# Naming PSUM pairs by a rough clock and ordering an attention stage by a plan string, in a fused attention and sine-MLP kernel

## The chip, the cores and the metric

One core of a Trainium2 chip. The metric is the device time of one execution in microseconds (us), the median of several runs; before: 469.61 us (469.1 to 469.65, 3 runs). A trace of one execution comes with each kernel; its span is some 2 us shorter than the timed run. Engine names: PE is TensorE, ACT ScalarE, DVE VectorE, POOL GpSimd, SP SyncE. The granted clock is the share of its full rate that TensorE was given, as the profile shows it; half clock is 0.50.

## The reference, cut to what matters

```python
def _attn_ref(q, k, v, g_q, g_k):            # 8 batches, 12 heads, 448 tokens, head width 64
    q_n, k_n = rmsnorm(q, g_q), rmsnorm(k, g_k)
    attn = softmax(q_n @ k_n.T / sqrt(64))
    return attn @ v
def _moe_ref(x, w_in, w_out, alpha):         # x: 3584 tokens x 768; 2048 hidden
    h = x @ w_in
    s = np.sin(alpha * h)
    g = h + s * s / (alpha + 1e-09)
    return g @ w_out
```

## The kernel before

For each batch there is an attention phase, then a first product (96 matmuls, 18.3 us; ACT, POOL and DVE turn it into g). The second product of batch b-1 has no attention of its own to wait for and is cut into steps that fill the attention phase of batch b on PE. Batch 0 has nothing to fill with and uses dummy matmuls.

The order of instructions is set by hand. All PSUM tiles (PSUM is the memory that this kernel's matmuls write to) are pairs of banks from one pool, in turn:

```python
psum = ctx.enter_context(tc.tile_pool(name="ps", bufs=4, space=bass.MemoryType.PSUM))
def bank_pair(name):
    return psum.tile([P, 2, 512], F32, tag="ps", name=name)
```

A score step S takes a pair until ACT has made the exponential; a value step A takes one until the denominator (two ACT passes) and the normalisation xT (two DVE multiplies) are done; an output tile takes one for 16 filler steps F and then until DVE has copied it out.

```python
def scores(c, j, warm=0):
    sc = bank_pair("sc")
    ...                                                     # 4 matmuls
    nc.scalar.activation(expT[c, j], sc[:, :, :S], ACT.Exp, scale=SCALE)
def attend(pi):
    av = bank_pair("av")
    ...                                                     # 28 matmuls: 7 key tiles, values and ones
    nc.scalar.activation(rec, av[:, 1, :S], ACT.Ln)
    nc.scalar.activation(rec, rec, ACT.Exp, scale=-1.0)
    ...                                                     # DVE: xT = av * rec, two halves
```

And the next batch's queries and keys are normed inside the attention phase, a chain over three engines and the DMA: squares and gain on POOL (steps 0, 1, 2), two reductions on DVE (3, 4), the inverse norm on ACT and the scaling on POOL (5), a transposing DMA (6). The list `at` says at which slot of the phase each step is issued; two such chunks run one after the other in a phase.

The softmax here doesn't subtract the row's maximum and nothing guards it: scores larger than these inputs give would overflow.

Of the kernel before, what the change touches and what calls it, by code (L numbers as in the profile page):

```python
# [32 lines left out]
def kernel(  # L33
# [38 lines left out]
    BUSY = (20, 8, 4, 2, 2)  # L72
# [10 lines left out]
    epool = ctx.enter_context(tc.tile_pool(name="expT", bufs=14))  # L83
# [5 lines left out]
    psum = ctx.enter_context(tc.tile_pool(name="ps", bufs=4, space=bass.MemoryType.PSUM))  # L89

    def bank_pair(name):
        return psum.tile([P, 2, 512], F32, tag="ps", name=name)
# [53 lines left out]
    def spread_g():  # L146

        nc.gpsimd.tensor_mul(g_rows[:, 2], g_rows[:, 0], g_rows[:, 1])
        ps = bank_pair("gps")
        nc.tensor.matmul(ps[:, 0, :D], ones_row, g_rows[:, 2], start=True, stop=True)  # L150
        nc.scalar.copy(gg[:, 0], ps[:, 0, :D])  # L151

    def spread_alpha():

        ps = bank_pair("aps")
        nc.tensor.matmul(ps[:, 0, :MT], small, ident_f32, start=True, stop=True)
        nc.vector.tensor_copy(alpha_sb[:, :, 0], ps[:, 0, :MT])
        nc.vector.reciprocal(inv_alpha_sb, alpha_sb)
# [12 lines left out]
    def keep_busy(n, rhs):  # L171


        ps = bank_pair("ps")
        for _ in range(n):
            nc.tensor.matmul(ps[:, 0, :rhs.shape[-1]], blank[:, :P], rhs, start=True, stop=True)

    qkT, expT, xT = {}, {}, {}

    def norm_tasks(ci):  # L180
# [6 lines left out]
        st.inv = {}  # L187
# [17 lines left out]
        def rsqrt(ws=slice(0, 2)):  # L205
            ln = npool.tile([P, 2, 2 * NJ], F32, tag="inv", name="inv")
            inv = bank_pair("inv")[:, :, :2 * NJ] if early else ln
            for w in range(2)[ws]:
                st.inv[w] = inv[:, w, :]
            nc.scalar.activation(ln[:, ws], st.ms[:, ws, :], ACT.Ln, scale=1.0 / D, bias=eps)  # L210
            nc.scalar.activation(inv[:, ws], ln[:, ws], ACT.Exp, scale=-0.5)

        def scale(w):
            eng = nc.vector if early else nc.gpsimd
            if st.n is None:
                st.n = npool.tile([P, 2, NJ, 2, D], BF16, tag="qkn", name="qkn")
            n, x = st.n[:, w], qk[ci][:, w].rearrange("p (hi j) d -> p hi j d", hi=2)
            inv = st.inv[w].rearrange("p (hi j) -> p hi j", hi=2)
            for hi in range(2):
                eng.tensor_mul(n[:, :, hi, :], x[:, hi], inv[:, hi].unsqueeze(2).to_broadcast([P, NJ, D]))  # L220

# [8 lines left out]
        def pe_transpose(pairs, ws=(0, 1), act=False):  # L230
            tp = psum.tile([P, 2, 1024], BF16, tag="ps", name="tp")
            for pp in pairs:
                pi, r = 2 * ci + pp, slice(pp * 64, pp * 64 + 64)
                if pi not in qkT:
                    qkT[pi] = tpool.tile([P, 2, S], BF16, tag="qkT", name="qkT")
                for w in ws:
                    for j in range(NJ):
                        c = w * S + j * REST
                        nc.tensor.transpose(tp[:, pp, c:c + REST], st.n[r, w, j], ident[r, r])
            for pp in pairs:  # L240
                out = qkT[2 * ci + pp][:, ws[0]:ws[-1] + 1].rearrange("p w s -> p (w s)")
                src = tp[:, pp, ws[0] * S:(ws[-1] + 1) * S]
                if act:
                    nc.scalar.copy(out, src)
                else:
                    nc.vector.tensor_copy(out, src)

# [6 lines left out]
    def scores(c, j, warm=0):  # L254

        sc = bank_pair("sc")
        for _ in range(warm):
            nc.tensor.matmul(sc[:, 0], blank[:, :P], blank, start=True, stop=True)
        for pp in range(2):
            for hi in range(2):  # L260
                qkt, r = qkT[2 * c + pp], slice(hi * 64, hi * 64 + 64)
                nc.tensor.matmul(sc[key_rows(pp, hi), pp, :S], qkt[r, 1, j * REST:(j + 1) * REST], qkt[r, 0, :],  # L262
                                 start=True, stop=True)
        expT[c, j] = epool.tile([P, 2, S], BF16, tag="expT", name="expT")
        nc.scalar.activation(expT[c, j], sc[:, :, :S], ACT.Exp, scale=SCALE)  # L265

    def attend(pi):
# [16 lines left out]
        for hi in range(2):  # L284
            r, o = slice(hi * 64, hi * 64 + 64), slice(64 - hi * 64, 128 - hi * 64)
            nc.vector.tensor_mul(xT[b][r, hp, :], av[r, 0, :S], rec[o, :])  # L286

    def snake(b, hps, m):
# [8 lines left out]
        def finish():  # L297
            nc.vector.scalar_tensor_tensor(  # L298
                g_sb[:, m, (b % 2) * S:(b % 2 + 1) * S], s2, inv_alpha_sb[:, m, :], hps, op0=ALU.mult, op1=ALU.add)
        return finish  # L300

    def first_product(b, beside):
# [10 lines left out]
        tiles = {}  # L313
        for kts in (range(KT - 2), [KT - 2], [KT - 1]):
            for i in range(EARLY):
                if i not in tiles:
                    tiles[i] = bank_pair("hps")
                for m in (2 * i, 2 * i + 1):
                    mm(tiles[i], m, kts)
        for i in range(MT // 2):  # L320
            if i >= EARLY:
                tiles[i] = bank_pair("hps")
                for m in (2 * i, 2 * i + 1):
                    mm(tiles[i], m, range(KT))
            for m in (2 * i, 2 * i + 1):
                late.append(snake(b, tiles[i][:, m % 2, :S], m))
# [4 lines left out]
        while late:  # L331
            late.popleft()()

    def second_product(b):
# [9 lines left out]
        for i, halves in units:  # L344
            st = {}

            def step(m, i=i, halves=halves, st=st):
# [4 lines left out]
                for k, half in enumerate(halves):  # L352
                    nc.tensor.matmul(st["ps"][:, k, :HALF], lhsT, w_out_sb[:, m, half * HALF:(half + 1) * HALF],  # L353
                                     start=(m == 0), stop=(m == MT - 1))
                if m == MT - 1:
                    n = len(halves)
                    osb = opool.tile([P, 2, HALF], F32, tag="osb", name="osb")
                    nc.vector.tensor_copy(osb[:, :n], st["ps"][:, :n, :HALF])  # L358
                    o = osb[:, :n].rearrange("p a d -> p (a d)")
# [51 lines left out]
    def beside_h(b):  # L411

        ci = NC * b + 5
        if ci >= NC * B:
            return {}
        return {0: [lambda: begin_norm(ci)], 1: [step_of(ci, 0)], 3: [step_of(ci, 1)], 4: [step_of(ci, 3)],
                5: [step_of(ci, 2)], 7: [step_of(ci, 4)]}

    FIRST, KEPT = 12, MT // 2
    for c in range(NC):  # L420
        for j in range(NJ):
            scores(c, j, BUSY[2 + c] if j % 2 else 0)
            if c and j in (1, 3):
                attend(2 * c - 2 + j // 2)
            if (c, j) == (0, 1):
                c1.rsqrt()
            if (c, j) == (0, 3):
                c2.square(0), c2.square(1)
                c2.fold_g()
                c1.scale(0), c1.scale(1)  # L430
                load_qk(NC)
            if (c, j) == (0, 4):
                c1.pe_transpose((0, 1))
                c2.reduce(0), c2.reduce(1)
            if (c, j) == (1, 0):
                c2.rsqrt()
                c2.scale(0), c2.scale(1)
                load_qk(NC + 1)
                load_w_out(0)
                begin_norm(NC)  # L440
                step_of(NC, 0, 1, 2)()
            if (c, j) == (1, 4):
                c2.pe_transpose((0, 1))
                step_of(NC, 3, 4)()
                v_parts = load_v(1)
                v_parts[0](), v_parts[1]()
                begin_norm(NC + 1)
                step_of(NC + 1, 0, 1, 2)()
            if (c, j) == (1, 6):
                step_of(NC, 5, 6)()  # L450
            if (c, j) == (2, 1):
                step_of(NC + 1, 3, 4)()
                v_parts[2](), v_parts[3]()
                load_w_out(1)
            if (c, j) == (2, 4):
                step_of(NC + 1, 5)()
    step_of(NC + 1, 6)()
    attend(NP - 2)
    attend(NP - 1)
    first_product(0, beside_h(0))  # L460

    visits = [(c, *x) for c in range(NC) for x in (((0, 1), 0), ((2, 3), 1), ((4, 5, 6), None))]
    for b in range(1, B):
        nc.scalar.preload_act_table_set(EXP_LN)
        fillers.extendleft(reversed(second_product(b - 1)))

        n_fill = len(fillers) - (KEPT if b % 2 == 0 else 0)

        at = [[] for _ in range(4 * NP + 8)]
# [3 lines left out]
        step_of(ci, 5)()  # L473
        at[s0].append(step_of(ci, 6))
# [8 lines left out]

        def beside_e(v, half):
            a, z = v * 4 * NP // len(visits), (v + 1) * 4 * NP // len(visits)
            mid = (a + z) // 2
            for slot in range(a, mid) if half == 0 else range(mid, z):
                for task in at[slot]:
                    task()

        fill(FIRST // 2 if b > 1 else 0)
        for n, (c, tiles, pp) in enumerate(visits):
            for j in tiles:
                scores(b * NC + c, j)
            if n == 0:
                fill(FIRST - (FIRST // 2 if b > 1 else 0))
            elif c and pp is not None:
                attend(b * NP + 2 * c - 2 + pp)
            beside_e(n, 0)
            left = n_fill - FIRST  # L500
            fill(left * (n + 1) // len(visits) - left * n // len(visits))
            beside_e(n, 1)
        attend(b * NP + NP - 2)
        attend(b * NP + NP - 1)
        for task in [task for slot in at[4 * NP:] for task in slot]:
            task()
# [31 lines left out]
```

## Time and profile before

| part of the span | us | PE idle in it |
|---|---|---|
| attention phase of batch 0, from the start | 45.6 | 8.0 after its first 13.9 us |
| attention phase of batch 1 | 34.9 | 3.9 |
| attention phases of batches 2 to 7, each | 35.7 | 2.1 |
| first products, each | 18.3 | none |
| last second product and store | 25.1 | at its end |

Read it as: PE is the bound, the first products are full, so only the attention phases can shrink. The lines are in the prediction. The phase lengths in this document are taken from the first and last first-product matmul in the timelines.

### The profile page before, as it was taken

The page shows a single profiled execution, that of the slowest core. Times are in us where ns is not written, and L with a number is a line of the kernel's source. Part 1 is how long each engine was busy: PE and PEld are TensorE (multiplying, and loading weights), DVE is VectorE, ACT ScalarE, POOL GpSimd, SP SyncE. Part 2 cuts the span into 40 slices and gives each one's busy share as a digit, 9 for nine tenths or more (in the row PEclk, how much of TensorE's full clock was granted, in tenths as well). Part 3 has the DMA queues.
Part 4 walks back from the last instruction along what each step waited for, and adds up shares of the span by engine and source line. Part 5 has one row for each costly group of instructions (what it writes and reads, how often), then busy time and mean ns, then how long its engine had stood idle before and what let it go on. Part 6 is the DMA issues. An engine that isn't in the chain of part 4 may idle for free.

```text
span 466.7 us, 9464 instructions
## 1 busy us (share of the span) xinstructions
PE 433.9 (93%) x3815; PEld 220.3 (47%) x3820; DVE 227.5 (49%) x331; ACT 342.8 (73%) x531; POOL 278.2 (60%) x262
## 2 busy tenths in 40 slices
PE   7768999899999999999999999999999999999996
PEld 2334544445544554445544555445544455445563
DVE  3764563537453473445545365435634464224521
ACT  4879877868876788767887688767887588876800
POOL 3868968828785368836788187854688276001400
PEclk9999999999999999999999999999999999999999
DMA  6999996490257905583055904668052901211023
GB/s 237 192 244 239 230 198 203 146 187 17 62 134 162 180 2 151 154 99 132 4 160 146 225 2 54 179 134 169 2 153 74 126 25 25 50 37 50 1 50 86
DMA packets 69296, 55.09 MB, mean 118 GB/s; under 512 B 41460, under 2 KB 65796, under 8 KB 69252
## 3 DMA queue, kind: packets, MB, share of 16 engines
q1 hardware_dynamic: 56690, 40.97, 34.6%
q0 software_dynamic: 11616, 11.81, 18.1%
q10 hardware_dynamic: 946, 1.70, 1.0%
q8 instruction: 30, 0.49, 0.4%
q14 instruction: 14, 0.11, 0.1%
HBM read 45.62 MB, written 11.01 MB: 121 GB/s over the span
## 4 chain that ended last, share of the span: by engine, by line
PE 66%; ACT 16%; DMA 6%; DVE 5%; issue 4%; POOL 2%; SPq 1%; DVEq 0%; POOLq 0%
PE hps L309 27%; PE ops L353 25%; ACT expT L265 11%; PE av L277 9%; PE sc L262 5%; DVE xT L286 4%; DMA qkT<-qkn 3%; ACT rec L281 2%; ACT rec L280 2%; DMA out_dram<-osb 1%; DMA g_rows<-in_g_q_dram 1%; POOL qkn L220 1%; SPq L226 1%; POOL qk L200 1%; SPq L102 1%
## 5 line engine op out<-in xcount | busy, mean ns | idle before, releaser
L265 ACT ACTIVATE expT<-sc 128x896 bf16<-128x896 f32 x168 | 144.0, 914 | 33.8 <-PE sc L262 33.7
L353 PE MATMUL ops<-w_out_sb,g_sb 128*128 128x384 bf16 x896 | 157.8, 327 | 0.0
L309 PE MATMUL hps<-xT,w_in_sb 128*128 128x448 bf16 x768 | 146.7, 353 | 0.0
L293 POOL TENSOR_TENSOR s<-s 128x448 f32<-128x448 f32 x64 | 59.2, 930 | 111.1 <-ACT s L290 100.1
L353 PEld LDWEIGHTS <-g_sb 128*128 128x128 bf16 x896 | 82.4, 98 | 70.6 <-issue 20.3
L298 DVE SCALAR_TENSOR_TENSOR g_sb<-s,inv_alpha_sb,hps 128x448 bf16<-128x448 f32 x128 | 81.3, 676 | 63.2 <-POOL s L293 63.2
L309 PEld LDWEIGHTS <-w_in_sb 128*128 128x128 bf16 x768 | 74.5, 98 | 71.5 <-issue 2.9
L286 DVE TENSOR_TENSOR xT<-av,rec 64x448 bf16<-64x448 f32 x96 | 59.7, 622 | 99.1 <-ACT rec L281 97.6
L220 POOL TENSOR_TENSOR qkn<-qk,inv 128x448 bf16<-128x448 f32 x84 | 76.1, 937 | 38.2 <-issue 21.0
L290 ACT ACTIVATE s<-hps,alpha_sb 128x448 f32<-128x448 f32 x128 | 74.5, 627 | 28.5 <-PE hps L309 26.7
L277 PE MATMUL av<-expT,vb 64*64 64x448 bf16 x672 | 71.8, 353 | 9.6 <-DVE xT L286 6.4
L197 POOL TENSOR_TENSOR sq<-qk 128x896 f32<-128x896 f32 x42 | 69.9, 1678 | 6.1 <-DVE ms L203 4.4
L277 PE MATMUL av<-expT,ones 64*64 64x448 bf16 x672 | 71.7, 353 | 0.0
L262 PE MATMUL sc<-qkT 64*64 64x448 bf16 x672 | 53.2, 365 | 10.1 <-DVE xT L286 7.3
L277 PEld LDWEIGHTS <-vb 64*64 64x64 bf16 x672 | 38.2, 107 | 34.4 <-issue 15.0
L203 DVE TENSOR_REDUCE ms<-sq 128x14 f32<-128x896 f32 x42 | 45.1, 1081 | 17.2 <-POOL sq L197 16.6
L200 POOL TENSOR_TENSOR qk<-qk,gg 128x896 f32<-128x896 f32 x24 | 50.2, 2090 | 5.3 <-ACT gg L151 3.3
L358 DVE COPY osb<-ops 128x768 f32<-128x768 f32 (+1 forms) x35 | 27.9, 797 | 43.9 <-PE ops L353 43.5
L280 ACT ACTIVATE rec<-av 128x448 f32<-128x448 f32 x48 | 26.1, 544 | 22.4 <-PE av L277 22.4
L295 ACT ACTIVATE s<-s 128x448 f32<-128x448 f32 x64 | 36.9, 577 | 2.8
L277 PEld LDWEIGHTS <-ones 64*64 64x64 bf16 x672 | 34.8, 107 | 4.2
L262 PEld LDWEIGHTS <-qkT 64*64 64x64 bf16 x672 | 15.4, 104 | 43.2 <-issue 29.1
(43 smaller groups left out, 138.0 us busy)
## 6 DMA issues: line engine op xcount, KB each, us to landing
qk<-in_q_dram SPq DMA_DIRECT2D x24, 448.0 KB, 5.9
qk<-in_k_dram SPq DMA_DIRECT2D x22, 448.0 KB, 7.7
out_dram<-osb SPq DMA_DIRECT2D x39, 192.0 KB, 4.7
vb<-in_v_dram POOLq DMA_DIRECT2D x32, 168.0 KB, 7.5
w_in_sb<-in_moe_w_in_dram POOLq DMA_DIRECT2D x2, 1536.0 KB, 18.2
w_out_sb<-in_moe_w_out_dram POOLq DMA_DIRECT2D x2, 1536.0 KB, 25.3
out_dram<-osb SPq DMA_DIRECT2D x26, 96.0 KB, 3.6
qk<-in_k_dram ACTq DMA_DIRECT2D x2, 448.0 KB, 6.0
```

Of the source, the lines that this page charges most:

```text
L197: nc.gpsimd.tensor_mul(st.sq[w], qk[ci][:, w], qk[ci][:, w])
L200: eng.tensor_mul(qk[ci][:, 0], qk[ci][:, 0], gg.to_broadcast([P, 2 * NJ, D]))
L220: eng.tensor_mul(n[:, :, hi, :], x[:, hi], inv[:, hi].unsqueeze(2).to_broadcast([P, NJ, D]))
L262: nc.tensor.matmul(sc[key_rows(pp, hi), pp, :S], qkt[r, 1, j * REST:(j + 1) * REST], qkt[r, 0, :], start=True, stop=True)
L265: nc.scalar.activation(expT[c, j], sc[:, :, :S], ACT.Exp, scale=SCALE)
L277: nc.tensor.matmul(av[o, part, :S], ones[r, :] if part else vb[b][r, hp, j, :], expT[pi // 2, j][r, pi % 2, :], start=(j == 0), stop=(j == ...
L286: nc.vector.tensor_mul(xT[b][r, hp, :], av[r, 0, :S], rec[o, :])
L290: nc.scalar.activation(s1, hps, ACT.Sin, scale=alpha_sb[:, m, :])
L293: nc.gpsimd.tensor_mul(s2, s1, s1)
L298: nc.vector.scalar_tensor_tensor(g_sb[:, m, (b % 2) * S:(b % 2 + 1) * S], s2, inv_alpha_sb[:, m, :], hps, op0=ALU.mult, op1=ALU.add)
L309: nc.tensor.matmul(ps[:, m % 2, :S], w_in_sb[:, kt, m * P:(m + 1) * P], x[:, kt, :], start=(kt == 0), stop=(kt == KT - 1))
L353: nc.tensor.matmul(st["ps"][:, k, :HALF], lhsT, w_out_sb[:, m, half * HALF:(half + 1) * HALF], start=(m == 0), stop=(m == MT - 1))
```

## The change

The intent: remove PE's waits for PSUM pairs, by naming the pair that should come free first, and by an order in which score steps run ahead. Of the diff (cut):

```diff
-    def bank_pair(name):
-        return psum.tile([P, 2, 512], F32, tag="ps", name=name)
+    def bank_pair(name, dtype=F32):
+        slot = min(free_at, key=free_at.get)
+        clock["pe"] = max(clock["pe"], free_at.pop(slot))
+        ps = psum.tile([P, 2, 2048 // mybir.dt.size(dtype)], dtype, tag=f"ps{slot}", name=name)
+        slot_of[id(ps)] = slot
+        return ps
...
+        give_back(sc, passes(0.2 + 0.2 * warm, 0.82) + 0.2)
...
+        give_back(av, passes(1.32, 1.06) + 1.4)
...
+                    give_back(st["ps"], passes() + 1.2)          # output tile
...
-    visits = [(c, *x) for c in range(NC) for x in (((0, 1), 0), ((2, 3), 1), ((4, 5, 6), None))]
+    PLAN = "6 SS 7 SS 7 SSS 8 SSS 8 SSAS 7 SS 5 SSASA 4 S 4 SSAAA"
...
-        step_of(ci, 5)()
-        at[s0].append(step_of(ci, 6))
+        at[s0].append(step_of(ci, 5))
+        at[s0 + 2].append(step_of(ci, 6))
```

(cut: the clock's bookkeeping at the other tiles; 17 exponential buffers instead of 14; one reduction moved behind the first product; the first two tiles of each first product interleaved; batch 0's phase rewritten with score steps ahead and most dummies gone.) The numbers in the plan are filler steps. A slot is now counted along the plan string.

More of the change, by code (lines that the diff above doesn't have):

```diff
@@ L71 @@
     HALF = D_MODEL // 2
-    BUSY = (20, 8, 4, 2, 2)
+    BUSY = (20, 8)
     ctx.enter_context(tc.manual_schedule())
@@ L82 @@
     tpool = ctx.enter_context(tc.tile_pool(name="qkT", bufs=8))
-    epool = ctx.enter_context(tc.tile_pool(name="expT", bufs=14))
+    epool = ctx.enter_context(tc.tile_pool(name="expT", bufs=17))
     rpool = ctx.enter_context(tc.tile_pool(name="rec", bufs=2))
@@ L88, with passes, give_back @@
     opool = ctx.enter_context(tc.tile_pool(name="osb", bufs=3))
-    psum = ctx.enter_context(tc.tile_pool(name="ps", bufs=4, space=bass.MemoryType.PSUM))
-    def bank_pair(name):
-        return psum.tile([P, 2, 512], F32, tag="ps", name=name)
+    psum = ctx.enter_context(tc.tile_pool(name="ps", bufs=1, space=bass.MemoryType.PSUM))
+    clock = {"pe": 0.0, "act": 0.0}
+    free_at = {slot: 0.0 for slot in range(4)}
+    slot_of = {}
+    def bank_pair(name, dtype=F32):
[4 more added lines that the diff above has]
+        return ps
+    def passes(pe=0.0, act=0.0):
+        clock["pe"] += pe
+        if act:
+            clock["act"] = max(clock["act"], clock["pe"] + 0.25) + act
+        return max(clock["pe"], clock["act"] if act else 0.0)
+    def give_back(ps, time):
+        free_at[slot_of.pop(id(ps))] = time
     qk, vb = {}, {}
@@ L151, in spread_g @@
         nc.scalar.copy(gg[:, 0], ps[:, 0, :D])
+        give_back(ps, passes(0.2, 0.2))
     def spread_alpha():
@@ L157, in spread_alpha @@
         nc.vector.tensor_copy(alpha_sb[:, :, 0], ps[:, 0, :MT])
+        give_back(ps, passes(0.2) + 0.5)
         nc.vector.reciprocal(inv_alpha_sb, alpha_sb)
@@ L176, in keep_busy @@
             nc.tensor.matmul(ps[:, 0, :rhs.shape[-1]], blank[:, :P], rhs, start=True, stop=True)
+        give_back(ps, passes(0.2 * n))
     qkT, expT, xT = {}, {}, {}
@@ L186, in norm_tasks @@
         st.ms = npool.tile([P, 2, 2 * NJ], F32, tag="ms", name="ms")
-        st.inv = {}
+        st.inv, st.inv_ps, st.scaled = {}, None, 0
         st.sq, st.n = {}, None
@@ L206, in rsqrt @@
             ln = npool.tile([P, 2, 2 * NJ], F32, tag="inv", name="inv")
-            inv = bank_pair("inv")[:, :, :2 * NJ] if early else ln
+            if early and st.inv_ps is None:
+                st.inv_ps = bank_pair("inv")
+            inv = st.inv_ps[:, :, :2 * NJ] if early else ln
             for w in range(2)[ws]:
@@ L220, in scale @@
                 eng.tensor_mul(n[:, :, hi, :], x[:, hi], inv[:, hi].unsqueeze(2).to_broadcast([P, NJ, D]))
+            st.scaled += 1
+            if early and st.scaled == 2:
+                give_back(st.inv_ps, passes() + 3.0)
         def transpose():
@@ L230, in pe_transpose @@
         def pe_transpose(pairs, ws=(0, 1), act=False):
-            tp = psum.tile([P, 2, 1024], BF16, tag="ps", name="tp")
+            tp = bank_pair("tp", BF16)
             for pp in pairs:
@@ L246, in pe_transpose @@
                     nc.vector.tensor_copy(out, src)
+            give_back(tp, passes(1.0) + 1.3)
         st.square, st.fold_g, st.reduce, st.rsqrt, st.scale = square, fold_g, reduce, rsqrt, scale
@@ L286, in attend, with snake @@
             nc.vector.tensor_mul(xT[b][r, hp, :], av[r, 0, :S], rec[o, :])
-    def snake(b, hps, m):
+        give_back(av, passes(1.32, 1.06) + 1.4)
+    def snake(b, ps, m):
+        hps = ps[:, m % 2, :S]
         s1 = spool.tile([P, S], F32, tag="s1", name="s1")
@@ L299, in finish @@
                 g_sb[:, m, (b % 2) * S:(b % 2 + 1) * S], s2, inv_alpha_sb[:, m, :], hps, op0=ALU.mult, op1=ALU.add)
+            if m % 2:
+                give_back(ps, passes() + (3.4 if m == MT - 1 else 1.8))
         return finish
@@ L312, in first_product @@
         EARLY = 2
-        tiles = {}
-        for kts in (range(KT - 2), [KT - 2], [KT - 1]):
-            for i in range(EARLY):
-                if i not in tiles:
-                    tiles[i] = bank_pair("hps")
-                for m in (2 * i, 2 * i + 1):
-                    mm(tiles[i], m, kts)
+        tiles = {i: bank_pair("hps") for i in range(EARLY)}
+        for kt in range(KT):
+            for m in range(2 * EARLY):
+                mm(tiles[m // 2], m, [kt])
+        passes(2.28 * EARLY)
         for i in range(MT // 2):
@@ L324, in first_product @@
                     mm(tiles[i], m, range(KT))
+                passes(2.28)
             for m in (2 * i, 2 * i + 1):
-                late.append(snake(b, tiles[i][:, m % 2, :S], m))
+                late.append(snake(b, tiles[i], m))
                 if len(late) > 1:
@@ L332, in first_product @@
             late.popleft()()
+        for task in beside.get(MT // 2, ()):
+            task()
     def second_product(b):
@@ L354, in step @@
                                      start=(m == 0), stop=(m == MT - 1))
+                passes(0.163 * len(halves))
                 if m == MT - 1:
@@ L416, in beside_h @@
         return {0: [lambda: begin_norm(ci)], 1: [step_of(ci, 0)], 3: [step_of(ci, 1)], 4: [step_of(ci, 3)],
-                5: [step_of(ci, 2)], 7: [step_of(ci, 4)]}
-    FIRST, KEPT = 12, MT // 2
-    for c in range(NC):
-        for j in range(NJ):
-            scores(c, j, BUSY[2 + c] if j % 2 else 0)
-            if c and j in (1, 3):
-                attend(2 * c - 2 + j // 2)
-            if (c, j) == (0, 1):
-                c1.rsqrt()
-            if (c, j) == (0, 3):
-                c2.square(0), c2.square(1)
-                c2.fold_g()
-                c1.scale(0), c1.scale(1)
-                load_qk(NC)
-            if (c, j) == (0, 4):
-                c1.pe_transpose((0, 1))
-                c2.reduce(0), c2.reduce(1)
-            if (c, j) == (1, 0):
-                c2.rsqrt()
-                c2.scale(0), c2.scale(1)
-                load_qk(NC + 1)
-                load_w_out(0)
-                begin_norm(NC)
-                step_of(NC, 0, 1, 2)()
-            if (c, j) == (1, 4):
-                c2.pe_transpose((0, 1))
-                step_of(NC, 3, 4)()
-                v_parts = load_v(1)
-                v_parts[0](), v_parts[1]()
-                begin_norm(NC + 1)
-                step_of(NC + 1, 0, 1, 2)()
-            if (c, j) == (1, 6):
-                step_of(NC, 5, 6)()
-            if (c, j) == (2, 1):
-                step_of(NC + 1, 3, 4)()
-                v_parts[2](), v_parts[3]()
-                load_w_out(1)
-            if (c, j) == (2, 4):
-                step_of(NC + 1, 5)()
@@ new lines, in beside_h, with stage @@
+                5: [step_of(ci, 2)], MT // 2: [step_of(ci, 4)]}
+    def stage(b):
+        tiles = deque((b * NC + c, j) for c in range(NC) for j in range(NJ))
+        pairs = deque(b * NP + p for p in range(NP))
+        return (lambda warm=0: scores(*tiles.popleft(), warm)), (lambda: attend(pairs.popleft()))
+    S_, A_ = stage(0)
+    S_(), S_(), S_()
+    c1.rsqrt()
+    S_(3)
+    c2.square(0), c2.square(1)
+    c2.fold_g()
+    c1.scale(0), c1.scale(1)
+    load_qk(NC)
+    S_(), S_(3), S_(4)
@@ new lines @@
+    c1.pe_transpose((0, 1))
+    c2.reduce(0), c2.reduce(1)
+    S_(), S_(3), A_(), S_()
+    c2.rsqrt()
+    c2.scale(0), c2.scale(1)
+    load_qk(NC + 1)
+    load_w_out(0)
+    begin_norm(NC)
+    step_of(NC, 0, 1, 2)()
+    S_(3), S_()
+    c2.pe_transpose((0, 1))
+    v_parts = load_v(1)
+    v_parts[0](), v_parts[1]()
+    begin_norm(NC + 1)
+    step_of(NC + 1, 0, 1, 2)()
+    S_(), S_(), S_(), S_(), S_()
+    step_of(NC, 3, 4)()
+    A_(), S_()
+    step_of(NC, 5, 6)()
+    A_(), S_()
+    step_of(NC + 1, 3, 4)()
@@ L457 @@
+    v_parts[2](), v_parts[3]()
+    load_w_out(1)
+    S_(), S_(), A_()
+    step_of(NC + 1, 5)()
+    A_(), A_()
     step_of(NC + 1, 6)()
-    attend(NP - 2)
-    attend(NP - 1)
     first_product(0, beside_h(0))
-    visits = [(c, *x) for c in range(NC) for x in (((0, 1), 0), ((2, 3), 1), ((4, 5, 6), None))]
+    PLAN = "6 SS 7 SS 7 SSS 8 SSS 8 SSAS 7 SS 5 SSASA 4 S 4 SSAAA"
+    KEPT, SLOTS = MT // 2, 24
+    plan = [x for word in PLAN.split() for x in ("F" * int(word) if word.isdigit() else word)]
@@ L463 @@
     for b in range(1, B):
         nc.scalar.preload_act_table_set(EXP_LN)
+        clock["act"] = clock["pe"] + 3.3
         fillers.extendleft(reversed(second_product(b - 1)))
         n_fill = len(fillers) - (KEPT if b % 2 == 0 else 0)
-        at = [[] for _ in range(4 * NP + 8)]
+        at = [[] for _ in range(SLOTS + 8)]
         s0, ci = 2, NC * b + 2
@@ L482 @@
                 at[s0 - 1 + n].append(part)
-        def beside_e(v, half):
-            a, z = v * 4 * NP // len(visits), (v + 1) * 4 * NP // len(visits)
-            mid = (a + z) // 2
-            for slot in range(a, mid) if half == 0 else range(mid, z):
+        S_, A_ = stage(b)
+        due = slot = 0
+        for n, x in enumerate(plan):
+            while slot * len(plan) <= n * SLOTS:
                 for task in at[slot]:
                     task()
-        fill(FIRST // 2 if b > 1 else 0)
-        for n, (c, tiles, pp) in enumerate(visits):
-            for j in tiles:
-                scores(b * NC + c, j)
-            if n == 0:
-                fill(FIRST - (FIRST // 2 if b > 1 else 0))
-            elif c and pp is not None:
-                attend(b * NP + 2 * c - 2 + pp)
-            beside_e(n, 0)
-            left = n_fill - FIRST
-            fill(left * (n + 1) // len(visits) - left * n // len(visits))
-            beside_e(n, 1)
-        attend(b * NP + NP - 2)
-        attend(b * NP + NP - 1)
-        for task in [task for slot in at[4 * NP:] for task in slot]:
-            task()
+                slot += 1
+            if x == "F":
+                due += n_fill
+                fill(due // plan.count("F"))
+                due %= plan.count("F")
+            else:
+                (S_ if x == "S" else A_)()
+        for tasks in at[slot:]:
+            for task in tasks:
+                task()
         first_product(b, beside_h(b))
```

## The prediction

> **What bounds the kernel now.** I read the page's busy times first, then the 18 windows cut at the phase borders, then the waits of TensorE, then the timelines of one middle phase.
>
> ```profile
> PE 433.9 (93%) x3815; PEld 220.3 (47%) x3820; DVE 227.5 (49%) x331; ACT 342.8 (73%) x531; POOL 278.2 (60%) x262
> ```
>
> TensorE (PE) is the bound: it is idle for 466.7 - 433.9 = 32.8 us. The windows say where (columns: window, its length, then busy us and instruction count of each engine, granted clock, DMA share, GB/s):
>
> ```profile
> 13.90:45.60 31.70, 23.70 (x328) 11.27 (x332) 20.34 (x32) 26.52 (x42) 23.60 (x22) 0.95 1.11 240
> 45.60:63.90 18.30, 18.30 (x102) 9.34 (x98) 10.91 (x17) 14.30 (x24) 16.74 (x16) 1.00 1.28 207
> 63.90:98.90 35.00, 31.14 (x350) 15.42 (x350) 15.98 (x24) 27.65 (x41) 25.09 (x24) 1.00 0.76 178
> 98.90:117.20 18.30, 18.30 (x102) 9.47 (x99) 10.88 (x17) 14.30 (x24) 11.55 (x10) 1.00 0.45 88
> 117.20:152.99 35.79, 33.67 (x365) 16.89 (x364) 16.29 (x22) 27.80 (x41) 25.04 (x24) 1.00 0.56 122
> ```
>
> The first product (18.3 us) leaves no TensorE idle. What is idle lies in the attention of batch 0 (8.0 us) and of batch 1 (3.9 us), and some 2.1 us in each of the six attention phases of batches 2 to 7. A period of a middle batch is 54.1 us. The waits of TensorE name the cause:
>
> ```profile
> PE sc L262 <- DVE xT L286: 7.3, 14, 0.6
> PE av L277 <- DVE xT L286: 6.4, 14, 0.7
> PE av L277 <- ACT expT L265: 3.0, 5, 1.1
> ...
> PE sc L262 <- DMA qkT<-qkn: 0.8, 1, 0.8
> ```
>
> 28 waits, 13.7 us, are of score and value matmuls for VectorE's normalisation (xT). Neither reads xT: they wait for the PSUM pair that xT still reads. The pool gives its four pairs in turn, so the fourth request after a value step ("av") gets the av pair, which lives longest (7 key tiles, two ScalarE passes, two VectorE multiplies), although another pair may have come free before. In the timeline of batch 2 (start, length, what, idle before):
>
> ```profile
> 131.37 0.57 PE L262 MATMUL sc<-qkT 64*64 64x448 bf16 x8
> 132.34 0.38 PE L277 MATMUL av<-expT,vb 64*64 64x448 bf16 x2 [0.40 <-DVE xT L286]
> ...
> 135.52 0.38 PE L262 MATMUL sc<-qkT 64*64 64x448 bf16 x4
> 136.40 0.91 PE L262 MATMUL sc<-qkT 64*64 64x448 bf16 x8 [0.50 <-DVE xT L286]
> 137.24 1.80 PE L353 MATMUL ops<-w_out_sb,g_sb 128*128 128x384 bf16 x10
> ```
>
> Start to start, an undisturbed run of three score steps in this phase takes 0.69 us; this one takes 137.24 - 135.52 = 1.72 us, so 1.03 us is lost, of which the idle column shows half. The pair of score steps before the value step takes 0.97 us against 0.60. Each pattern comes twice per phase: 2 x 1.03 + 0.37 + 0.39 = 2.8 us lost.
>
> **What the Trainium skill says.** "PSUM — Partial Sum Buffer", Specifications (TRN2): 8 banks of 2 KiB per partition; a pair is two banks, so there are four pairs and no fifth. The trace agrees as far as it goes: the waits are for pairs. "Perfetto Trace Analysis", Optimization Strategy: the same gap repeated on the engine that should be saturated can mean too little PSUM for the next tile; here it is 0.4, 0.5, 0.4, 0.5 us in every middle phase. "PSUM — Partial Sum Buffer", Engine vs sequencer instructions: ScalarE and VectorE take their queues strictly in order; my first rival rests on it. "TensorE: Matmul & The Clock Gate", Part 1: idle TensorE drops to half clock after an idle window of about 3.4 us, hence the dummy matmuls; the trace shows clock 0.95 in the first attention phase and some value steps there at twice their usual spacing.
>
> **The change, part by part.** I call F one second-product step (two matmuls of 384 columns), S a score step, A a value step.
>
> 1. Pairs named by a rough clock. It adds no instruction. It takes the pair whose promised release is earliest instead of the next in turn, and should remove the 2.8 us per middle phase.
>
> 2. The plan string. The 56 F, 21 S and 6 A remain; only the order changes: twelve S before the first A instead of nine, and the last three A together. (14 exponential buffers would not do for this; there are now 17.) Walking it with start-to-start times of batch 2: 12 matmuls of F take 2.04 us, so 0.163 each plus 0.1 per run; S is 0.25, three 0.69; A is 1.45, a pair 2.77, so three 4.17. Nine F runs give 56 x 0.325 + 0.9 = 19.1; S runs 5.5; A 3 x 1.45 + 4.17 = 8.5. Sum 33.1 us where the old phase takes 152.92 - 117.03 = 35.9: a gain of 2.8 if nothing waits.
>
> 3. But one wait is new. In the built order ScalarE's second inverse norm (for the next batch's first chunk) now stands before the eighth exponential; before, it stood behind the ninth and its own value step. The old timelines of ScalarE and VectorE:
>
> ```profile
> 121.02 0.23 ACT L211 ACTIVATE inv<-inv 128x28 f32<-128x28 f32 x1
> ...
> 130.81 0.30 ACT L210 ACTIVATE inv<-ms,eps 128x28 f32<-128x28 f32 x1
> ```
>
> ```profile
> 126.67 1.09 DVE L203 TENSOR_REDUCE ms<-sq 128x14 f32<-128x896 f32 x1 [2.68 <-POOL sq L197]
> 128.31 1.09 DVE L203 TENSOR_REDUCE ms<-sq 128x14 f32<-128x896 f32 x1 [0.55 <-POOL sq L197]
> ```
>
> From the end of the first inverse norm (121.25) through GpSimd's four scalings and two squares to the end of the second reduction (129.40) are 8.15 us. In the new order the first inverse norm comes after one exponential and a reduction moved behind the last gate operation, and ends near 4.8 us into the phase (before: 4.2), so the second can't begin before 12.95. Until then ScalarE has done seven exponentials (the last near 10.7) and stands idle for about 2.2 us. Score step 8, issued at 11.2, is evacuated at 13.5 to 14.3. The built allocation gives the third output tile, in every one of batches 2 to 6, the very pair of score step 8; TensorE reaches it at 13.2 and waits 1.1 to 1.2 us. After that I find ScalarE just ahead of TensorE to the end (last exponential at 31.7, the fifth value step needs it at about 32.5). Phase: about 34.4 us, a gain of 1.5.
>
> 4. The first phase. Score steps run ahead, most dummies go (TensorE was not short there: ScalarE was busy 26.5 of 31.7 us). Walking ScalarE's queue at 0.82 us per exponential and 1.12 per reciprocal pair, with the second and third chunk's transposes still blocking TensorE's queue, the first product begins near 44.4 instead of 45.6: 1.2 us. But the second batch's keys come by transposing DMA:
>
> ```profile
> 48.99 15.97 DMA qkT<-qkn
> 65.00 0.57 PE sc L262 x6
> ```
>
> GpSimd finishes the scaling that feeds it at 44.8, held by the load of the fourth chunk's keys (landed at 37.5), and its own order is unchanged. So the first score step of batch 1 remains at about 65.0. What is gained before that is only that five F steps (1.7 us) now stand ahead of it. Walking batch 1 (48 F, so shorter F runs, again the inverse norm stall, costing 1.5) from there, its end is at 95.8 instead of 98.9: a gain of 3.1 over everything up to there.
>
> 5. Sum. 3.1 up to the end of batch 1; batches 2 to 6: 5 x 1.5 = 7.5; batch 7, which norms no next batch and so has no stall: 2.7. The tail (20.8 us of second product, then store) is unchanged, and the first products too, being full. Total 13.3; 469.6 - 13.3 = 456.3.
>
> **The rivals.**
> A: the new stall costs nothing, because score steps have run ahead and the third output tile is reached later than I think. Then batches 1 to 6 gain 1.2 more each: 449. For it: TensorE's wait is only a difference of two estimates, 14.3 - 13.2. Against it: 2.2 us of ScalarE idle must go somewhere, ScalarE having 25.5 us of exponentials, reciprocals and norms after its table load.
> B: ScalarE becomes the bound. Three S per 2.6 us of F ask 2.5 us of exponentials, so it has no reserve there, and any stall is carried to the three A at the end, which need the last exponential. The rough clock charges no time for switches or inverse norms, so its promises slip by 1 to 3 us per phase and pairs may be named badly. Then half of the gain goes: 462 to 464. For it: ScalarE is busy 27.8 of 35.8 us already, and starts 3.3 us late for the table load. Against it: 6 us of slack.
> C: the first phase loses by a cold TensorE, its dummies gone: value steps at double time, up to 4 us. Against it: the DMA transposes hide everything before 65.0 up to about 1 us. Only beyond that does it count: 457 to 459.
>
> **Range and chances.** My walk is likelier to miss a wait than to invent one, so I shift slightly up: 456.5. Rival A sets the low end with a little luck missing, 450.5; half of B and some of C the high end, 462.5. A gain of over 2% means under 460.2: I give it 0.80; within 2%, 0.19; slower, 0.01, since no work is added and TensorE's waits on xT have no reason to grow.
>
> **What would show it.** Step 1 is right if waits of sc and av on xT fall from 13.7 us to under 3. Step 2: a middle attention phase of 33 to 35 us, with first products still 18.3. Step 3: in batches 2 to 6 ScalarE idles about 2 us before the inverse norm at L235, released by the reduction, and TensorE waits about 1 us for an exponential at an output tile; batch 7 is over 1 us shorter than they are. Step 4: the first score step of batch 1 within 1.5 us of 65.0, released by the DMA. Wrong if middle phases stay above 35.3, if the waits move from xT to expT at equal size, or if batch 1's keys land much later.

## The result

467.94 us (466.71 to 468.07, 4 runs) against 469.51 us for the kernel before in the same rounds; the ratio is 0.9962, with a 95% interval of 0.9944 to 0.998. So it is the same within 2%, and 5.4 us above the predicted range of 450.5 to 462.5. A ratio here is the mean time of one kernel's runs over the mean of the other's in the same rounds, so not quite the ratio of the medians quoted.

The windows of the changed kernel, cut at its own phase borders (columns as in the prediction: window, length, busy us and count of PE, PE's weight loads, DVE, ACT, POOL, then granted clock, DMA share, GB/s):

```profile
13.80:47.10 33.30, 26.41 (x322) 12.78 (x324) 20.17 (x32) 26.36 (x41) 24.32 (x23) 0.80 1.11 236
47.10:65.40 18.30, 18.30 (x101) 9.49 (x98) 10.93 (x17) 14.30 (x24) 15.87 (x15) 1.00 1.31 212
65.40:105.10 39.70, 32.88 (x350) 16.77 (x348) 15.92 (x23) 27.42 (x41) 25.07 (x24) 0.91 0.81 155
123.40:158.50 35.10, 32.57 (x365) 17.14 (x362) 16.16 (x21) 27.41 (x41) 25.05 (x24) 1.00 0.63 129
390.60:422.60 32.00, 32.00 (x365) 16.74 (x363) 11.94 (x17) 26.56 (x37) 4.67 (x6) 1.00 0.24 59
```

The gain and the losses stand side by side. Batch 7 (last line) is 3.7 us shorter than before and PE is busy in all of it. Batches 2 to 6 gain 0.6 us each. Batch 1 is 4.7 us longer than before, batch 0 1.5 us. Sum: 1.5 + 4.7 - 5 x 0.6 - 3.7 = -0.5, and the span fell from 466.7 to 466.1.

The waits of PE (us in total, times, longest), answering to the xT lines of before, and one of ACT:

```profile
ACT inv L235 <- DVE ms L226: 28.2, 13, 3.2
...
PE sc L291 <- ACT expT L294: 7.5, 8, 1.1
PE sc L291 <- DVE osb L394: 6.1, 2, 4.0
...
PE ops L388 <- ACT expT L294: 5.3, 5, 1.1
```

No wait on xT is left. In their place stand waits for exponentials, and two long ones for output copies. The ACT line has the source of the first kind: inverse norms that stand in ACT's queue until DVE's reduction is there, 28.2 us in total.

Batch 2, timelines of PE and of ACT:

```profile
137.68 1.46 PE L388 MATMUL ops<-w_out_sb,g_sb 128*128 128x384 bf16 x8 [1.05 <-ACT expT L294]
...
147.15 0.38 PE L291 MATMUL sc<-qkT 64*64 64x448 bf16 x4 [1.06 <-ACT expT L294]
147.95 0.38 PE L307 MATMUL av<-expT,vb 64*64 64x448 bf16 x2 [0.42 <-ACT expT L294]
```

```profile
136.25 0.32 ACT L235 ACTIVATE inv<-ms,eps 128x28 f32<-128x28 f32 x1 [2.21 <-DVE ms L226]
...
145.72 0.32 ACT L235 ACTIVATE inv<-ms,eps 128x28 f32<-128x28 f32 x1 [2.63 <-DVE ms L226]
```

Twice per phase ACT stands idle for over 2 us at an inverse norm, with exponentials queued behind it, and PE waits for one of those exponentials until 1.4 us after the norm has begun. Batch 7 has no such norms and no wait.

Batch 1, timelines of PE, DVE and POOL:

```profile
72.56 0.57 PE L291 MATMUL sc<-qkT 64*64 64x448 bf16 x8
77.12 0.59 PE L291 MATMUL sc<-qkT 64*64 64x448 bf16 x4 [3.99 <-DVE osb L394]
77.64 4.66 PE L388 MATMUL ops<-w_out_sb,g_sb 128*128 128x384 bf16 x14
```

```profile
75.51 1.09 DVE L226 TENSOR_REDUCE ms<-sq 128x14 f32<-128x896 f32 x1 [5.57 <-POOL sq L220]
76.52 0.55 DVE L394 COPY osb<-ops 128x384 f32<-128x384 f32 x1
```

```profile
73.80 3.31 POOL L220 TENSOR_TENSOR sq<-qk 128x896 f32<-128x896 f32 x2
```

The output tile was complete before 72.6, but its copy stands in DVE's queue behind a reduction, which waits for POOL's square; DVE idles 5.57 us, for the last 2.9 us of them with a copy that could run. The third score step of the run has been given that tile's pair and waits 4.0 us. Then the 14 filler matmuls take 4.6 us; in batch 2 fourteen take 2.4. The granted clock was 0.50 in that stretch, so the wait is paid a second time, by 2.2 us:

```profile
77.20:82.30 5.10, 5.10 (x22) 2.08 (x25) 1.03 (x1) 1.35 (x3) 4.97 (x5) 0.50 0.91 216
```

The second long wait (2.1 us, at 91.4) is also for a copy: that one stands behind xT and a reduction, of which only xT had been waiting, for ACT.

### The profile page after: what moved, and what is told of

Its sections match the earlier page's. It is cut to its first block, busy times and chain, and to the rows that moved or that the text cites. A ratio compares the mean times of both kernels' runs of the same rounds, so it can differ in the third digit from the quotient of the medians.

```text
span 466.1 us, 9452 instructions
## 1 busy us (share of the span) xinstructions
PE 431.0 (92%) x3810; PEld 224.4 (48%) x3812; DVE 227.7 (49%) x331; ACT 340.3 (73%) x531; POOL 278.1 (60%) x262
## 4 chain that ended last, share of the span: by engine, by line
PE 62%; ACT 11%; POOL 10%; DVE 9%; issue 5%; DMA 2%; SPq 0%; POOLq 0%; DVEq 0%
PE hps L343 31%; PE ops L388 14%; PE av L307 12%; ACT expT L294 7%; DVE ms L226 5%; POOL qkn L245 4%; POOL sq L220 4%; PE sc L291 4%; DVE xT L316 1%; ACT inv L235 1%; POOL s L325 1%; DVE g_sb L330 1%; PE sc L287 1%; DMA qkT<-qkn 1%; ACT inv L236 1%
## 5 line engine op out<-in xcount | busy, mean ns | idle before, releaser
L388 PE MATMUL ops<-w_out_sb,g_sb 128*128 128x384 bf16 x896 | 159.9, 330 | 5.3 <-ACT expT L294 5.3
L388 PEld LDWEIGHTS <-g_sb 128*128 128x128 bf16 x896 | 83.5, 98 | 77.9 <-issue 27.4
L307 PE MATMUL av<-expT,vb 64*64 64x448 bf16 x672 | 70.7, 356 | 3.6 <-ACT expT L294 3.6
L394 DVE COPY osb<-ops 128x768 f32<-128x768 f32 (+1 forms) x35 | 27.9, 798 | 47.1 <-PE ops L388 46.3
L307 PEld LDWEIGHTS <-vb 64*64 64x64 bf16 x672 | 39.5, 109 | 15.9 <-issue 5.4
L307 PEld LDWEIGHTS <-ones 64*64 64x64 bf16 x672 | 38.6, 109 | 10.6
L291 PEld LDWEIGHTS <-qkT 64*64 64x64 bf16 x672 | 16.4, 107 | 45.1 <-issue 40.4
## 6 DMA issues: line engine op xcount, KB each, us to landing
w_in_sb<-in_moe_w_in_dram POOLq DMA_DIRECT2D x2, 1536.0 KB, 19.3
```

Source lines behind the costliest of these rows:

```text
L291: nc.tensor.matmul(sc[key_rows(pp, hi), pp, :S], qkt[r, 1, j * REST:(j + 1) * REST], qkt[r, 0, :], start=True, stop=True)
L307: nc.tensor.matmul(av[o, part, :S], ones[r, :] if part else vb[b][r, hp, j, :], expT[pi // 2, j][r, pi % 2, :], start=(j == 0), stop=(j == ...
L388: nc.tensor.matmul(st["ps"][:, k, :HALF], lhsT, w_out_sb[:, m, half * HALF:(half + 1) * HALF], start=(m == 0), stop=(m == MT - 1))
```

## The experiments

My theory after the result (1): the plan is good, but it issues the norm steps too early for POOL, and whatever waits for POOL at the head of an in-order queue holds up PSUM evacuations behind it, on ACT in batches 1 to 6 and on DVE in batch 1. The rival (2): the rough clock names the wrong pairs and so makes the waits. Further open: what naming gives at all, and what the new phase of batch 0 costs. Eleven runs of nine kernels were made (two kernels ran twice), all correct. Times are medians; "before" is the kernel before in the same rounds.

| kernel | us | before | ratio (95%) | phases of batch 0, 1, 2 to 6, 7 |
|---|---|---|---|---|
| changed | 467.94 | 469.51 | 0.9962 (0.9944-0.9980) | 47.1, 39.6, 35.1, 32.0 |
| late_norms | 443.13 | 468.57 | 0.9455 (0.9441-0.9469) | 45.1, 32.0, 32.0, 32.0 |
| slots_only | 478.76 | 468.57 | 1.0215 (1.0200-1.0230) | 47.2, 36.1, 37.05, 37.0 |
| plan_only | 464.20 | 468.57 | 0.9902 (0.9865-0.9939) | 47.3, 39.6, 34.6, 32.0 |
| old_first | 469.03 | 468.57 | 0.9996 (0.9961-1.0031) | 48.1, 40.3, 35.1, 32.0 |
| late_rot | 441.84 | 469.59 | 0.9421 (0.9386-0.9455) | 43.6, 31.3, 32.0, 32.0 |
| slots_promise | 473.49 | 469.59 | 1.0090 (1.0058-1.0122) | 49.3, 35.0, 36.6 or 35.7, 35.7 |
| late_warm | 445.09 | 469.59 | 0.9483 (0.9455-0.9512) | 47.4, 32.0, 32.0, 32.0 |
| late_first | 472.47 | 469.59 | 1.0068 (1.0041-1.0094) | 45.5, 35.4, 36.7 to 38.2, 32.0 |
| late_rot_b | 442.10 | 469.46 | 0.9415 (0.9400-0.9430) | 45.5, 31.3, 32.0, 32.0 |
| late_norms_b | 442.42 | 469.46 | 0.9430 (0.9416-0.9443) | 45.7, 32.0, 32.0, 32.0 |
| late_rot_old_first | 443.56 | 469.46 | 0.9448 (0.9431-0.9465) | 45.5, 31.3, 32.0, 32.0 |

The first products take 18.3 us in all of these traces but for the first one of late_rot (19.3) and of slots_promise (18.6).

### late_norms: the norm steps later, nothing else

```diff
-                for n, step in ((4, 3), (5, 4), (6, 5), (8, 6)):
+                for n, step in ((7, 3), (8, 4), (9, 5), (11, 6)):
                     at[s0 + n].append(step_of(ci, step))
-                s0 += 8
+                s0 += 9
```

> Edit: in the changed kernel the next batches' norm steps (two reductions, inverse norm with scaling, transpose) are placed 3, 3, 3 and 3 slots later, and the second chunk starts one slot later; nothing else. Theory 1 (work that waits for GpSimd's squares was placed too early, and blocks the in-order queues behind it: the reductions block VectorE's output copies in batch 1, the inverse norms block ScalarE's exponentials in batches 1 to 6): the 6.1 us of score waits on the output copy in batch 1 go, batch 1's attention phase falls from 39.7 to about 32.5 us (its half-clock stretch after the long wait goes too), batches 2 to 6 from 35.2 to 32.1 as batch 7 already has; total 444 to 449 us. Rival (the rough clock names bad pairs): the waits stay, only their releaser changes; total 464 or more.

443.13 us, ratio 0.9455, slightly under the expected range. Every attention phase from batch 1 on took 32.0 us. The same two windows as above (batch 1, batch 2), and the waits of PE between 63.5 and 415 us, of which these are all:

```profile
63.40:95.40 32.00, 30.13 (x349) 15.79 (x346) 15.77 (x23) 27.32 (x41) 24.84 (x24) 1.00 0.81 180
113.80:145.80 32.00, 32.00 (x364) 16.74 (x363) 16.18 (x21) 27.33 (x41) 24.86 (x24) 1.00 0.55 131
```

```profile
PE sc L291 <- DVE osb L394: 1.0, 1, 1.0
PE ops L388 <- DVE osb L394: 0.7, 1, 0.7
```

The rule that names the pairs and the plan are those of the changed kernel; beside the norm steps only the loads of v fall two slots later. So theory 1 holds, and rival 2 falls as the main cause of the lost gain: 7.6 us came back in batch 1, 3.1 in each of batches 2 to 6 (2.0 more came in batch 0, which the edit does not touch; see below). ACT, DVE and POOL do the same work in the same phase, only in 3 us less.

### late_first: only the first of the two norm chunks later

```diff
+                d = 3 if s0 == 2 else -1
                 for n, step in ((4, 3), (5, 4), (6, 5), (8, 6)):
-                    at[s0 + n].append(step_of(ci, step))
-                s0 += 8
+                    at[s0 + n + d].append(step_of(ci, step))
+                s0 += 9
```

> Edit: as late_norms for the first of the two chunks only; the second chunk's reductions, inverse norm and transposes stay in their old slots. The two stalls of a middle phase are one chain through GpSimd: with the first chunk's scaling later, the second chunk's squares end about 1 us later still (near 22 us into the phase, where ScalarE meets its inverse norm near 18). Theory: the first wait (output on exponential, 1.05 us) goes, the second grows from 1.5 to 2.5 us or more, so middle phases end between 34.3 and 35.3, not at 33.5. If the stalls were independent: 33.5 us. Batch 1 loses its 4 us wait, so total 455 to 463.

The chain is as expected: the first wait is gone and the second grew. In batch 2 ACT idled 4.20 us at the second inverse norm, and PE waited 2.63 us and 0.42 us. But the phases took 36.7 to 38.2 us, not 34.3 to 35.3. The timeline of PE and a window after the wait:

```profile
141.65 0.38 PE L291 MATMUL sc<-qkT 64*64 64x448 bf16 x4 [2.63 <-ACT expT L294]
```

```profile
142.40:145.40 3.00, 2.94 (x32) 1.82 (x35) 0.00 (x0) 1.69 (x4) 3.00 (x5) 0.50 0.51 115
```

32.0 + 2.63 + 0.42 = 35.1; of the remaining 1.9 us of the 37.0 some 1.5 are the 3.0 us at half clock (0.50) after the wait, in which the value step runs at twice its spacing. Waits of 1.05 us, in the changed kernel, left the clock at 1.00. In batch 1 the 4.0 us wait went, as expected, but a wait of 2.96 us for another output copy came, again with the half clock behind it; the total of 472.47 us misses the expected 455 to 463.

### slots_only and slots_promise: naming without the plan

slots_only takes the changed kernel and puts the old order back in all phases. slots_promise then changes one number:

```diff
-                    give_back(st["ps"], passes() + 1.2)
+                    give_back(st["ps"], passes() + 3.5)
```

> Edit: pairs named by the rough clock, but the old order in the first phase and in all attention phases. If the fixed turn of the pairs was what cost the kernel before its 13.7 us of waits on xT: those waits fall under 3 us, middle attention phases go from 35.8 to about 33.2 us, total 450 to 455. If a guessed clock can't name pairs well without the order planned for it: waits move to exponentials or output copies and the total stays above 463.

> Edit: slots_only (old order, named pairs) with one number changed: the output pair is promised 3.5 us after its last matmul instead of 1.2. Theory: slots_only is slow because the promise is too early (the copy stands behind the normalisations in VectorE's queue and ended 3.6 to 3.9 us after the unit's last matmul), so score steps get a pair that is not free; with the later promise the 19 us of score waits on output copies fall under 5 us and the middle phases from 37.05 to 35 or less, total 465 or less. Rival: naming by a clock can't work in the old order at all; waits move to xT or exponentials and the total stays above 472.

In both the hoped-for gain failed to come and the second reading held. With the old order, naming made the kernel 2.1% slower. The waits of score steps on xT fell from 7.3 to 0.6 us, those of value steps stayed (5.7 us), and 19.1 us of score waits on output copies came. The timelines of DVE and PE in a middle phase of slots_only:

```profile
193.20 1.26 DVE L316 TENSOR_TENSOR xT<-av,rec 64x448 bf16<-64x448 f32 x2 [2.90 <-ACT rec L311]
194.49 0.96 DVE L394 COPY osb<-ops 128x768 f32<-128x768 f32 x1
```

```profile
195.50 0.57 PE L291 MATMUL sc<-qkT 64*64 64x448 bf16 x8 [1.49 <-DVE osb L394]
```

The clock promised the output's pair 1.2 us after its last matmul; the copy waits behind xT in DVE's queue, so a score step that could have had the value step's pair at 194.5 got the output's at 195.5 (which pair each tile got is read from the program as built). With the later promise the waits on output copies vanished, and the waits on xT returned: 7.3 us in 14 and 6.0 us in 13 waits, nearly the numbers of the kernel before. Its middle phases are 35.7 like before, or 36.6.

Why no name could help is in the timelines of before (DVE):

```profile
135.09 1.26 DVE L286 TENSOR_TENSOR xT<-av,rec 64x448 bf16<-64x448 f32 x2 [2.90 <-ACT rec L281]
136.38 0.96 DVE L358 COPY osb<-ops 128x768 f32<-128x768 f32 x1
```

At 135.7 us one pair holds the output tile that is being filled; one the output tile before it, whose copy ran from 136.38 to 137.34; one the value step, whose xT ran until 136.35; one the first score step of the run, just issued. The second score step waits for the first of the four to be released, and that is the value step's pair, freed by xT. The pool's turn had already picked that pair. At the other kind of wait, near 132 us, it is the same: an output tile being filled, two score steps whose exponentials begin at 131.8, and the value step before, whose xT ends at 132.20.

### plan_only and late_rot: the plan without naming

Both put the pool of four in turn back; plan_only into the changed kernel, late_rot into late_norms. The edit is in both the same:

```diff
-        slot = min(free_at, key=free_at.get)
-        ...
+        return psum.tile([P, 2, 2048 // mybir.dt.size(dtype)], dtype, tag="ps", name=name)
```

> Edit: the changed kernel, but its pairs given in turn again, four buffers of one pool. If naming the pairs matters: waits on xT come back, now also in batch 7, whose attention phase goes from 32.1 to 34 or more; total 472 or more. If the order alone had removed the waits: total 466 to 469.

> Edit: late_norms with its pairs given in turn by one pool of four. If naming the pairs gives nothing beside the new order (plan_only ran batch 7 in the same 32.0 us as the named kernel): every attention phase from batch 1 on stays within 0.5 us of 32.0 and the total within 2 us of 443.1. If naming is what lets the plan run without waits once the norms are out of the way: waits on xT come back, phases above 33.5, total above 452.

plan_only ran in 464.20 us, below either expectation: no wait on xT at all and batch 7 again 32.0 us. Its longest waits of PE:

```profile
PE sc L287 <- ACT expT L290: 7.4, 8, 1.0
PE ops L384 <- ACT expT L290: 5.3, 5, 1.1
PE sc L287 <- DVE osb L390: 5.1, 2, 4.2
```

They are nearly those of the changed kernel, so the naming did not make them. Each middle phase is 0.5 us shorter than with named pairs: the wait of 0.42 us of a value step on an exponential, after the second stall, is not there in any of the five. That much of rival 2 is true. late_rot ran in 441.84 us. The plan removes the waits on xT by itself, and the norm steps are worth over 22 us with named pairs (467.94 to 443.13) and without (464.20 to 441.84). Because late_norms and late_rot had run on different chips, I ran both once more on one chip.

> late_rot once more, on the same chip as the next two. If naming the pairs is worth nothing: within 0.5% of late_norms_b.

> late_norms once more on the same chip. If naming the pairs is worth something beside the new order, this is faster than late_rot_b by more than 1 us; if it is worth nothing, within 0.5%; in the earlier runs, on two chips, it was 1.3 us slower.

442.10 against 442.42 us, intervals overlapping, middle phases equal to 0.02 us. Naming the pairs is worth nothing here. In batch 1 turn-taking is even 0.8 us shorter (31.2 against 32.0).

### old_first, late_warm and late_rot_old_first: batch 0

> Edit: the changed kernel with the first phase in the old order and with its dummy matmuls. Theory: the new first phase costs 1.6 us because TensorE falls to half clock in it (its last three value steps took 5.78 us against 3.97 later): first product starts near 45.6 instead of 47.2, batch 1 keeps its 39.7 us, total about 466.3. Rival: the new first phase also spoils batch 1 (by where its loads and norms fall): batch 1's attention phase falls below 37 us as well and the total below 464.

> Edit: late_norms plus 20 dummy matmuls ahead of the last eight score steps of the first phase (two ahead of four, three ahead of four). If the first phase loses time to the half clock (granted clock 0.89 up to 47 us in late_norms, 0.85 in the changed kernel): the clock there rises over 0.93, the first product starts at 44.5 or earlier instead of 45.1, total 441 to 443. If ScalarE's queue sets its length: the clock rises and nothing else does, total 442.5 to 444.5.

> Edit: late_rot with the first phase in the old order, with its dummy matmuls. If the new first phase, scores ahead, is worth what I predicted for it (1.2 us): this is 1 to 2 us slower than late_rot_b. If it is worth nothing: the same within 1 us; the attention phases from batch 2 on stay at 32.0 us in either case.

old_first put the old order and dummies of batch 0 back into the changed kernel, late_rot_old_first into late_rot; late_warm added dummies to late_norms ahead of score steps:

```diff
-    S_(), S_(), S_(), S_(), S_()
+    S_(), S_(2), S_(2), S_(2), S_(2)
...
-    A_(), S_()
+    A_(), S_(3)
...
```

old_first left batch 1 as bad as it was (40.3 us), so the new first phase did not spoil it, but its batch 0 was longer too (48.1 us, where 45.6 was expected). Its pairs are still named, and the naming goes with this: the old first order took 45.6 and 45.5 us with pairs in turn (before, late_rot_old_first), but 48.1, 47.2 and 49.3 us with named pairs (old_first, slots_only, slots_promise), one trace each; why is not shown. late_warm raised the clock of the first 47 us from 0.89 to 0.93 as intended, and its batch 0 took 47.4 us instead of 45.1: a miss under both readings. Its four timed runs (444.97 to 445.66) lie above all those of late_norms and late_norms_b (442.35 to 443.67). It shows that these dummies buy nothing; that they delay the scores behind them and so ACT is my reading, not shown apart. late_rot_old_first had the same batch 0 in its trace as late_rot_b (45.5 and 45.5) and was 1.5 us slower in the timed runs; its interval just misses that of late_rot_b. So the new first phase is worth about 1.5 us in these runs, hardly clear of noise, and one trace each doesn't show where.

What adds to this: four kernels share batch 0 instruction for instruction (the changed one, late_norms, late_norms_b, late_first), and it took 47.1, 45.1, 45.7 and 45.5 us. In the changed kernel's trace its last three value steps took from 41.33 to 47.11, 5.8 us, at about twice the usual spacing for part of it; in late_norms from 40.98 to 45.08, 4.1 us. The granted clock was 0.70 in the first stretch and 1.00 in the second, so 1.7 of these 2.0 us are half clock that fell differently. The 1.5 us by which batch 0 seems longer than before is within this spread; what sets the half clock there stays open.

## Why the prediction was wrong

It said 456.3 by its sum and 467.94 came. By its own terms: end of batch 1 at 105.1 instead of 95.8 (+9.3); batches 2 to 6 at 35.1 instead of 34.4 (+3.5 over five); batch 7 at 32.0 instead of 33.1 (-1.1). Together +11.7.

- **Part 4 failed, and it is most of the error.** "Walking batch 1 ... again the inverse norm stall, costing 1.5": I walked ACT's queue there and not DVE's. In batch 1 output tiles are half as long, so copies come more often, and two of them are held up in DVE's queue, one by a reduction that waits for POOL (PE waits 4.0 us), one by xT and a reduction (2.1 us), with 2.2 us of half clock after the first. late_norms removed it by moving the norm steps, and batch 1 then ended at 95.4; the walk, with a stall of 1.5 us in it, had 95.8. The 1.2 us gain in batch 0 did not come either (45.6 before, 47.1 in this trace), mostly for the half clock named above (1.7 us). The gate at 65.0 by the key DMA doesn't show in this trace, whose first score step came at 67.0 and waited for nothing; it does in late_norms and late_rot, where the DMA releases the rest of the first score step at 65.39 and 65.40. That part of the walk was right.
- **Part 3 was right in mechanism and one stall short.** Predicted: second inverse norm not before 12.95 us into the phase, ACT idle 2.2, PE waiting 1.1 to 1.2 at the third output tile. Measured: 136.25 - 123.42 = 12.83, 2.21 and 1.05. But the third inverse norm, of the second chunk, stalls ACT again for 2.63 us and costs PE 1.06 + 0.42. The prediction found ScalarE "just ahead of TensorE to the end" after the second; in the built order the third norm stands before the 14th exponential, too early for its reduction, and that was not checked as the second was. The prediction's own sign of being wrong came true: in batches 2 to 6 the waits on xT were replaced by 12.7 us of waits on exponentials.
- **Part 2 was right, its size too small.** "33.1 us ... if nothing waits": 32.0, in batch 7 and in all phases of late_norms from batch 1 on. By its own terms, in batch 2 of late_norms, start to start: F 19.1 us as predicted, S 4.9 instead of 5.5, A 8.15 instead of 8.5.
- **Part 1 was wrong in its reason.** "Another pair may have come free before" is not so: all four were in use and the turn gave the first to be released. (Nor was it the "fourth request": between the value steps at 128.19 and 132.34 only two score steps take pairs, so the third request gets the pair, as an output tile in the making stands outside the turn.) The waits on xT did fall to zero, as the check asked for, but plan_only has them at zero without naming. The check could not tell the two parts apart.
- **The rivals.** None was it. A (stall costs nothing) is excluded by the 1.05 us. B (ACT the bound) named the right place and a wrong cause: in late_norms PE is busy in all of the 32.0 us and ACT in 27.3, so ACT has room. Its badly named pairs are worth the 0.5 us of a middle phase by which plan_only is shorter. C (cold batch 0) shows in the trace with 1.7 us, but kernels with the same batch 0 don't all show it.

The version that beats both kernels is late_rot: the plan, norm steps 3 slots later, pairs in turn. 441.84 and 442.10 us in two sets of rounds, 5.8% under the kernel before.

## What to carry to other kernels

When an order is compressed, the steps of a slower side chain must be moved with it: a step issued before its input is there costs nothing by itself, but in the in-order queues of ACT and DVE it held every PSUM evacuation (exponential or copy) behind it. Walk each in-order queue, not only the one of the bound and the one you suspect, and check each instance of a step. Before changing how buffers are assigned, count how many are in use at the wait; if all are, only the order can help.

## What the Trainium skill lacked or had wrong

- "TensorE: Matmul & The Clock Gate", Part 1 gives an idle window of about 3.4 us for the drop to half clock, in windows that run freely. The two states agree (0.50 and 1.00 here). But in late_first, batch 1, PE ran no matmul for 2.96 us (81.7 to 84.6) and the next 3.0 us had clock 0.50. After batch 0, all nine PE waits of 2.6 us or more in the traces here, six of them under 3 us, were followed by the half clock (0.50 to 0.67 over the next 3 us), waits up to 1.5 us never were, and of two waits of 2.11 us one was (0.70) and one was not (1.00). A plan that takes every gap under 3.4 us for safe would have been wrong here.
- "Perfetto Trace Analysis", Optimization Strategy says that a repeated gap can mean too little PSUM for the next tile, and names buffer count and tile sizes. The sign was true at the old waits (four of four pairs in use); naming was not the cure (slots_only, 1.0215), and more buffers were not tried. Reordering, which that passage doesn't name, made the same four pairs enough (32.0 us, no waits).
- "PSUM — Partial Sum Buffer", Engine vs sequencer instructions states the strict order of ACT's and DVE's queues, and the traces agree. What that order can cost PSUM I found on no page I read: an output copy of 0.55 us, whose tile was complete before 72.6, began at 76.52 behind a reduction that waited for POOL, and PE waited 3.99 us for its pair.
